# Attention with a mixture layer on one core: the written order of the first eleven stretches, replaced by another

## The chip, the core and the metric

The kernel runs on one core of a Trainium2 chip. The metric is the device time of one execution in microseconds (us); lower is better. Times of the kernel before: a median of 790.81 us over three runs (790.41 to 791.25). The engines are called by the names that the profile uses: PE (matmuls; PEld are its weight loads), DVE (vector), ACT (activation), POOL, and SP, which in this kernel only issues DMAs. ACT and POOL can issue DMAs as well.

## The reference, cut to what matters

```
xn = layernorm(A_x)                            # 2048 tokens x 640
q  = xn @ wq                                   # 32 heads of 192
k, v = the last 512 cached rows of each head   # given, not projected
p  = softmax(q @ k.T * 192**-0.5)              # per head, 2048 x 512
s  = (p @ v, heads joined) @ wo                # 2048 x 640
g  = silu(xn + the update of the two tokens with the highest xn @ w_r)   # a gated MLP on those two
out = A_x + s * g
```

Everything is bfloat16 outside the accumulators. Inputs and outputs lie in HBM.

## The kernel before, in words

**Tiles and units.** The 2048 tokens are 16 tiles of 128. Heads are taken in pairs p (two heads, 2 x 192 columns), and two pairs make a group g of four heads. A *step* i is (group, block of 512 tokens, pair): i = 0 and 1 are pairs 0 and 1 of tokens 0 to 511, i = 2 and 3 the same pairs for tokens 512 to 1023, and so on. A *unit* n is 128 tokens of a step for both heads of the pair: units 4i to 4i+3 belong to step i, 256 in all. Units are worked on in *stretches*: stretch 0 has units 0 and 1, stretch 1 units 2 and 3, and from there on each has three (stretch 2 has 4, 5, 6; stretch 10 has 28, 29, 30). There are 86.

**No scheduler.** The order on each engine is the order in which the program records its operations. Each engine runs its list strictly in that order. Semaphores let an instruction wait for data or for a buffer that another engine still holds. For stretches 11 to 84 a formula (stretch(), line 837) writes the list, the last one is the text LAST, and for the start and the stretches 0 to 10 it is written by hand as a text of tokens, FIRST (line 867). first() (line 668) turns each token into instructions. The tokens, with their lines in the profile:

- `x.t.lo.hi` loads token tiles lo to hi of block t (L101); `k`, `wq`, `v`, `wo` load keys, weights and values (L120 and L124, L112, L133, L140). A trailing `a` puts the load's issue on ACT's queue, otherwise SP issues it.
- `bn.n.h` (L172, L174 on DVE) or `as.n` (L242, L243 on ACT) take the layernorm statistics of tile n; `sq`, `rc` (L232, L235) or `pw.lo.hi` (L220 to L223 on POOL) make the reciprocal deviations; `ap.n.v` or `ap.n.g` writes the normalised tile (L260 on DVE, L258 on POOL); `sx` and `ex` load ACT's tables for square root and exponential.
- `turn.n` transposes tile n on PE (L267) and copies it out on the engine named; `kt` does so for the first keys (L282, L289; copies L283 on ACT, L290 on DVE). `xT.lo.hi` transposes normalised tiles by a DMA that SP issues (L271), and `kT.p` does it for keys (L128).
- `z.1` is a matmul on zeros that only keeps PE going at the start (L695).
- `q.i.c` is chunk c (128 columns of three) of the query projection of step i, five matmuls (L317); with lo and hi only for those tiles. A trailing `g` takes its PSUM buffer from the pool of six (p) instead of the pool of two (f). `qe` copies it out, scaled (L309 on ACT, L307 on DVE).
- `S.j` is the scores of stretch j: two matmuls of 128 rows for each unit (L331), then two of 64 rows (L338). Six p buffers are taken by three units, so S.j must wait for whatever held them last.
- `M.n.h` is the row maximum (L346, DVE), `E.n.h` the exponential with its row sum (L353, ACT), `P.n` the transpose of the exponentials by a DMA that SP issues (L358), `R.j` the reciprocals of the sums (L362).
- `O.n` is the product with the values, eight matmuls (L372), `Oe` its scaled copy (L385 on ACT, L387 on DVE), `T.j` its transpose by DMA from SP (L393).
- `W.w` is the output projection of 128 tokens for a group, twelve matmuls in two halves (L420); `We` copies it into the accumulator (L432).

**What the order has to respect.** PE, DVE, ACT, POOL and SP each have a list of their own, and a token that stands early for one engine holds up all later tokens of that engine. A DMA that SP issues waits, besides its data, for the landing of the one eight places ahead in the same list. The two f buffers are used in turn by `q`, `O` and `turn` without `g`; the next use waits for the copy-out of the last but one. Buffers of exponentials (5), their transposes (6) and attention outputs (3) are taken in turn as well.

Of the kernel before, what the change touches and what calls it, by code (L numbers as in the profile page):

```python
# [925 lines left out]
```

## Time and profile before

| | |
|---|---|
| median of the runs shown | 790.81 us (790.41 to 791.25) |
| time of the profiled execution | 789.15 us |
| its span in the profile | 787.4 us, so 1.75 us lie around it |
| mean granted PE clock | 0.999 |
| DVE busy | 621.7 us (79%) |
| ACT busy | 479.4 us (61%) |
| POOL busy | 179.5 us (23%) |
| moved by DMA | 143.80 MB, 421358 of 453133 packets under 512 B |

Busy time of PE is a union of pipelined matmuls: a matmul of 512 columns counts about 379 ns and follows the one before it after 216 ns, so a stall shorter than the rest of a matmul doesn't show as idle time. Stalls of PE are therefore read from the length of a group of equal matmuls against the same group elsewhere. A DMA's duration in the timeline is that of its issue on SP (SPq) or ACT (ACTq); the view of DMAs gives the time from issue to landing.

### The profile page before, as it was taken

How to read it: one execution, taken by the hardware profiler on the slowest of the kernel's cores; microseconds unless marked ns; L12 is line 12 of the kernel's file. 1: busy time of each engine (PE TensorE's matmuls, PEld its weight loads, DVE VectorE, ACT ScalarE, POOL GpSimd, SP SyncE). 2: the span in 40 equal slices, each digit the busy share in tenths (PEclk: the TensorE clock that was granted, in tenths of full speed). 3: DMA queues.
4: the chain of work that ended last, by engine and by line, in shares of the span. 5: the costliest groups of instructions: out<-in, count | busy, mean ns of one | idle time of the engine just before them, and what ended most of it. 6: DMA issues, size and time to landing. Idle time of an engine off the chain costs nothing.

```text
span 787.4 us, 15694 instructions
## 1 busy us (share of the span) xinstructions
PE 781.8 (99%) x5767; PEld 482.8 (61%) x5767; DVE 621.7 (79%) x1238; ACT 479.4 (61%) x1299; POOL 179.5 (23%) x198
## 2 busy tenths in 40 slices
PE   8999999999999999999999999999999999999998
PEld 4566656666666666566666655666566666556666
DVE  7976678988888777777777777777788988777786
ACT  8975766565556655565665556565667865565652
POOL 3230000000010000000000699960000000165966
PEclk9999999999999999999999999999999999999999
DMA  9999998899889999999998899779997799997996
GB/s 262 214 202 229 204 199 132 164 175 202 166 147 219 184 195 217 142 221 198 191 222 144 181 180 188 158 141 174 202 172 138 143 193 184 183 194 152 177 167 148
DMA packets 453133, 143.80 MB, mean 183 GB/s; under 512 B 421358, under 2 KB 452720, under 8 KB 453056
## 3 DMA queue, kind: packets, MB, share of 16 engines
q1 hardware_dynamic: 447696, 138.04, 94.0%
q10 hardware_dynamic: 4672, 3.08, 1.4%
q0 software_dynamic: 688, 1.68, 0.9%
q8 instruction: 45, 0.74, 0.4%
q14 instruction: 32, 0.26, 0.1%
HBM read 39.98 MB, written 2.62 MB: 54 GB/s over the span
## 4 chain that ended last, share of the span: by engine, by line
PE 95%; DMA 2%; DVE 1%; ACT 1%; issue 0%; SPq 0%; POOL 0%; DVEq 0%
PE q_ps L317 26%; PE w_ps L420 26%; PE o_ps L372 21%; PE sc L331 14%; PE sc L338 8%; DMA oT<-o_sb 1%; DMA x_in<-in_A_x_dram 1%; ACT pexp L353 1%; DVE nm L346 0%; DVE stats L172 0%; POOL fin_o L447 0%; PE gu_ps L590 0%; ACT o_sb L385 0%; PE y_ps L627 0%; DVE fin_t L445 0%
## 5 line engine op out<-in xcount | busy, mean ns | idle before, releaser
L353 ACT ACTIVATE pexp<-sc,nm 128x512 bf16<-128x512 f32 x512 | 348.5, 697 | 264.1 <-issue 231.7
L346 DVE TENSOR_REDUCE nm<-sc 128x1 f32<-128x512 f32 x512 | 314.9, 682 | 70.9 <-PE sc L338 70.7
L317 PE MATMUL q_ps<-xnT,wq_p 128*128 128x512 bf16 (+1 forms) x985 | 225.4, 374 | 0.5 <-DMA wq_p<-in_A_wq_dram 0.5
L420 PE MATMUL w_ps<-wo_g,oT 128*128 128x320 bf16 (+1 forms) x1542 | 223.0, 298 | 0.1
L420 PEld LDWEIGHTS <-oT 128*128 128x128 bf16 x1542 | 150.4, 98 | 69.5 <-DMA oT<-o_sb 0.4
L372 PE MATMUL o_ps<-v_sb,pT 128*128 128x192 bf16 x2048 | 184.8, 246 | 0.0
L372 PEld LDWEIGHTS <-pT 128*128 128x128 bf16 x2048 | 171.4, 98 | 14.0 <-issue 2.8
L317 PEld LDWEIGHTS <-wq_p 128*128 128x128 bf16 x985 | 89.7, 98 | 122.8 <-issue 33.3
L387 DVE TENSOR_TENSOR o_sb<-o_ps,lsum 128x384 bf16<-128x384 f32 x240 | 132.0, 556 | 41.3 <-PE o_ps L372 22.7
L331 PE MATMUL sc<-kT,qT 128*128 128x512 bf16 x512 | 125.5, 379 | 0.1
L434 DVE TENSOR_TENSOR s_acc<-s_acc,w_ps 128x320 f32<-128x320 f32 x192 | 92.5, 483 | 30.7 <-PE w_ps L420 30.7
L353 ACT ACTIVATION_READ_ACCUMULATOR pexp<-sc,nm 128x1 f32 x512 | 110.2, 215 | 0.0
L309 ACT ACTIVATE qT<-q_ps 128x512 bf16<-128x512 f32 (+1 forms) x180 | 98.7, 604 | 0.0
L331 PEld LDWEIGHTS <-qT 128*128 128x128 bf16 x512 | 48.5, 98 | 42.0 <-issue 1.5
L338 PE MATMUL sc<-kT,qT 64*128 64x512 bf16 x512 | 70.2, 380 | 0.0
L338 PEld LDWEIGHTS <-qT 64*128 64x128 bf16 x512 | 18.0, 94 | 46.7 <-issue 35.8
L664 POOL TENSOR_TENSOR s_acc<-s_acc,xn 128x640 f32<-128x640 f32 x16 | 22.9, 1434 | 103.0 <-DVE s_acc L434 102.9
L643 POOL TENSOR_TENSOR xn<-xn,yh 128x640 bf16<-128x640 bf16 x32 | 44.6, 1394 | 2.7
L633 POOL DMA_DIRECT2D y_d<-y_sb x4 | 2.2, 544 | 181.2 <-DVE y_sb L630 181.2
L510 POOL DMA_DIRECT2D c_d<-cand x1 | 0.7, 725 | 162.8 <-DVE cand L508 162.8
L665 POOL TENSOR_TENSOR s_acc<-s_acc,x_fin 128x640 f32<-128x640 f32 x16 | 22.4, 1400 | 61.4 <-DVE s_acc L434 54.3
L642 POOL TENSOR_SCALAR yh<-y_bc,oh 128x640 bf16<-128x640 bf16 x32 | 25.6, 800 | 5.2 <-DMA y_bc<-y_d 3.6
(110 smaller groups left out, 234.1 us busy)
## 6 DMA issues: line engine op xcount, KB each, us to landing
wo_g<-in_A_wo_dram SPq DMA_DIRECT2D x15, 480.0 KB, 4.3
wq_p<-in_A_wq_dram SPq DMA_DIRECT2D x14, 480.0 KB, 4.6
v_sb<-in_A_v_cache_dram SPq DMA_DIRECT2D x15, 384.0 KB, 4.3
k_raw<-in_A_k_cache_dram SPq DMA_DIRECT2D x28, 192.0 KB, 3.2
pT<-pexp SPq DMA_TRANSPOSE x256, 3.6
x_fin<-in_A_x_dram SPq DMA_DIRECT2D x16, 160.0 KB, 2.7
wgu<-in_B_w_gate_dram SPq DMA_DIRECT2D x15, 128.0 KB, 3.3
wgu<-in_B_w_up_dram SPq DMA_DIRECT2D x15, 128.0 KB, 3.6
```

The source lines that it names most:

```text
L309: nc.scalar.activation(out=out, in_=in_, func=ACT.Copy, scale=scale)
L317: nc.tensor.matmul(q_ps, lhsT=wq_of[g * PAIRS + pr][:, dc, c * P:(c + 1) * P], rhs=xnT[:, t5 * 4 + lo:t5 * 4 + hi, dc, :], start=(dc == 0) ...
L331: nc.tensor.matmul(sc_of[n][hh], lhsT=qT_of[i][:, 2 * hh, u * P:(u + 1) * P], rhs=kp[:, :, 2 * hh, :], start=True, stop=False)
L338: nc.tensor.matmul(sc_of[n][hh], lhsT=qT_of[i][hs, 1, u * P:(u + 1) * P], rhs=kp[hs, :, 1, :], start=False, stop=True)
L346: nc.vector.tensor_reduce(out=nm_of[j][:, c:c + 1], in_=sc_of[n][hh], axis=AX.X, op=ALU.max, negate=True)
L353: nc.scalar.activation(out=pe_of[n][:, hh, :], in_=sc_of[n][hh], func=ACT.Exp, bias=nm_of[j][:, c:c + 1], scale=1.0, accum_out=l_of[j][:, ...
L372: nc.tensor.matmul(ps[:, hh, :], lhsT=pT_of[n][:, hh, jj, :], rhs=v_sb[:, hh, jj, :], start=(jj == 0), stop=(jj == NJ - 1))
L387: nc.vector.tensor_tensor(out=osb_of[j][:, m], in0=ps, in1=l_of[j][:, 2 * m:2 * m + 2].unsqueeze(2).to_broadcast([P, 2, Dh]), op=ALU.mult)
L420: nc.tensor.matmul(w_ps, lhsT=oT_of[j][:, stretches[j].index(n), c % 3, :], rhs=wo_of[g][:, c, lo:hi], start=(c == 0), stop=(c == CPG - 1))
L434: nc.vector.tensor_tensor(out=acc, in0=acc, in1=w_ps, op=ALU.add)
L642: nc.gpsimd.tensor_scalar(out=yh, in0=M["y_bc"][:, j, :], scalar1=M["oh"][:, n, j:j + 1], scalar2=0.0, op0=ALU.mult, op1=ALU.add)
L643: nc.gpsimd.tensor_tensor(out=xn[:, n, :], in0=xn[:, n, :], in1=yh, op=ALU.add)
```

## The change

The text FIRST is replaced by another text; nothing else is. The sets of tokens agree but for details: tile 0 is turned with a p buffer and copied by ACT, tiles 2 and 3 are copied by ACT as well, and `kt.0` is copied by DVE; the load of tiles 2 and 3 is made of two loads (`x.0.2.3`, `x.0.3.4`), which stand next to each other in SP's list, so that six DMAs are issued up to `wq.0` and not five; the two loads `wo.0.0` and `wo.0.1` stand apart in the text, with no other SP token between them; loads that ACT issued (`wq.2`, `wq.3`, `v.2`, `k.3.0`, `k.3.1`, `k.2.0`, `wo.1.0`) are issued by SP; `T.9` is one DMA instead of two; tiles 12 and 15 exchange the engines of their statistics, and tiles 8, 12, 14 and 15 those that normalise them (DVE and POOL); and several copies out of PSUM change between DVE and ACT, or the buffer pool of their matmuls between f and p. Everything from stretch 11 on is recorded as before. In the diff one line is the start or a stretch:

```diff
--- before.py
+++ after.py
@@ -865,18 +865,18 @@
 
     J0 = 11
     FIRST = """
-z.1 z.1 z.1 sx z.1 z.1 x.0.0.2 x.0.2.4 as.1 k.0.1 k.0.0 bn.0.0 bn.0.1 bn.3.0 sq.0.1 sq.1.2 as.2 rc.0.1 rc.1.2 wq.0 x.1.1.2 ap.0.v ex ap.1.v bn.3.1 pw.2.4 turn.0.v turn.1.1.v kt.0.a kt.1.v q.0.0.0.2.g qe.0.0.0.2.a ap.3.g bn.5.0 x.1.0.1 x.1.3.4 x.1.2.3 q.0.1.0.2.g k.1.1 bn.5.1 qe.0.1.0.2.a q.0.2.0.2.g k.1.0 qe.0.2.0.2.a turn.3.1.a as.6 ap.2.v bn.7.0 bn.7.1 turn.2.v 
-S.0 bn.4.0 v.0 bn.4.1 wq.1 q.0.0.2.4.g qe.0.0.2.4.a x.2.0.4 kT.1 M.0.0 E.0.0 pw.4.8 q.0.2.2.4.g M.0.1 qe.0.2.2.4.v E.0.1 P.0 q.0.1.2.4 qe.0.1.2.4.a M.1.0 M.1.1 E.1.0 E.1.1 ap.4.v 
-S.1 q.1.2 ap.5.g M.2.0 ap.7.g E.2.0 M.2.1 q.1.0.2.4 ap.6.g xT.4.6 q.1.0.0.2.g bn.10.0 qe.1.2.a M.3.0 M.3.1 R.0 bn.10.1 xT.6.8 E.2.1 qe.1.0.0.2.a qe.1.0.2.4.a q.1.1 P.2 bn.11.0 O.0 bn.11.1 bn.8.0 E.3.0 E.3.1 qe.1.1.a Oe.0.v P.1 bn.8.1 
-S.2 x.3.0.4 v.1 q.2.1.0.2 as.9 M.4.0 M.4.1 q.2.0 M.6.0 E.4.0 pw.8.12 E.4.1 q.2.2.g M.5.0 qe.2.1.0.2.a E.5.0 qe.2.0.v M.6.1 ap.10.g E.6.0 ap.9.g P.3 E.6.1 M.5.1 q.3.1 qe.2.2.v ap.8.v R.1 ap.11.g O.2 qe.3.1.v Oe.2.v E.5.1 
-S.3 M.8.0 M.7.0 P.4 P.5 M.8.1 q.2.1.2.4 M.7.1 R.2 xT.8.10 M.9.0 as.13 bn.15.0 M.9.1 E.8.0 E.7.0 E.8.1 q.3.2 bn.14.0 xT.10.12 E.7.1 P.6 qe.2.1.2.4.a q.3.0.g qe.3.0.a qe.3.2.v E.9.0 E.9.1 O.1.g O.5.g O.4.g Oe.4.a Oe.1.v P.8 as.12 Oe.5.v O.3 
-S.4 P.7 bn.15.1 M.10.0 q.4.1 M.11.0 M.12.0 M.11.1 Oe.3.a q.4.0 P.9 M.10.1 qe.4.1.v E.10.0 M.12.1 E.11.0 T.0 E.11.1 q.5.0.g E.10.1 wo.0.0 wo.0.1 T.2.0.1 E.12.0 E.12.1 R.3 qe.4.0.a O.8.g O.7 P.10 Oe.7.a qe.5.0.v T.1 Oe.8.v R.4 bn.14.1 pw.12.16 
-S.5 ap.12.g O.6 M.13.0 P.11 E.13.0 M.15.1 Oe.6.a M.15.0 E.15.0 E.15.1 q.4.2 M.13.1 P.12 q.5.2.g M.14.1 M.14.0 qe.4.2.v O.9 E.13.1 Oe.9.a qe.5.2.v E.14.0 W.0 We.0.v E.14.1 
-S.6 M.17.0 P.13 M.17.1 ap.14.g M.16.1 O.10 M.18.1 Oe.10.a M.16.0 ap.13.g E.17.0 q.5.1 E.17.1 qe.5.1.v T.2.1.3 E.16.0 R.5 O.12 O.11.g Oe.11.a M.18.0 E.18.0 Oe.12.a E.16.1 W.1 O.13.g We.1.v E.18.1 ap.15.g xT.13.16 xT.12.13 W.2 We.2.v P.15 Oe.13.a 
-S.7 q.6.1 M.19.1 M.19.0 E.19.0 M.20.0 q.6.0 qe.6.0.v P.14 T.4 M.21.0 M.20.1 M.21.1 E.19.1 T.3 q.6.2.g k.2.1.a qe.6.1.a O.14 O.15.g R.6 E.20.0 q.7.1.g E.20.1 Oe.14.a P.17 qe.6.2.a E.21.0 Oe.15.v q.7.0 P.16 E.21.1 P.19 W.3 P.18 W.4 qe.7.1.v R.7 qe.7.0.v We.3.v O.19 We.4.a wq.2.a 
-S.8 wq.3.a O.16 Oe.19.v M.22.0 v.2.a M.23.1 E.22.0 Oe.16.v k.3.0.a M.23.0 P.20 E.23.0 wo.1.0.a E.23.1 k.3.1.a T.5 M.22.1 M.24.0 P.21 q.7.2 E.24.0 O.17 Oe.17.v E.22.1 P.22 k.2.0.a W.5 qe.7.2.v M.24.1 We.5.a O.20 P.23 W.6 O.21 We.6.a E.24.1 Oe.20.a Oe.21.a O.18.g Oe.18.v P.24 
-S.9 M.25.0 M.27.1 M.25.1 M.27.0 q.8.1 E.25.0 E.25.1 q.9.0 T.6 M.26.0 qe.8.1.v W.7 E.27.0 E.27.1 E.26.0 M.26.1 R.8 We.7.v P.25 qe.9.0.v E.26.1 q.8.0 T.7 
-S.10 P.27 qe.8.0.v M.28.0 E.28.0 O.22 O.23 Oe.22.a M.29.0 O.24.g P.26 q.8.2 M.28.1 M.29.1 R.9 Oe.23.v O.25 E.28.1 M.30.0 E.29.0 W.9 Oe.25.v E.30.0 E.29.1 qe.8.2.a kT.2 Oe.24.a P.28 M.30.1 kT.3 We.9.a W.8 E.30.1 We.8.v O.26.g P.29 O.27.g T.8 P.30 Oe.26.a wo.1.1 Oe.27.a v.3 T.9.2.3 T.9.0.2
+z.1 z.1 z.1 z.1 x.0.0.2 bn.0.0 x.0.2.3 sx as.1 bn.0.1 sq.0.1 sq.1.2 rc.0.1 x.0.3.4 rc.1.2 ap.0.v ap.1.v bn.3.0 k.0.0 z.1 as.2 turn.0.1.a bn.3.1 k.0.1 wq.0 turn.1.v kt.0.v kt.1.v x.1.3.4 pw.2.4 q.0.0.0.2.g ex ap.2.v q.0.1.0.2.g qe.0.0.0.2.a qe.0.1.0.2.a turn.2.a q.0.2.0.2.g ap.3.g bn.7.0 qe.0.2.0.2.a x.1.1.2 bn.7.1 turn.3.a 
+S.0 bn.5.0 bn.5.1 x.1.0.1 x.1.2.3 q.0.2.2.4.g k.1.1 as.6 bn.4.0 bn.4.1 k.1.0 M.0.0 wq.1 q.0.0.2.4.g E.0.0 v.0 M.0.1 E.0.1 qe.0.0.2.4.v qe.0.2.2.4.v x.2.0.4 q.0.1.2.4 q.1.0.0.2 qe.0.1.2.4.a qe.1.0.0.2.a pw.4.8 M.1.0 E.1.0 ap.4.v ap.5.g M.1.1 kT.1 P.0 E.1.1 
+S.1 M.2.0 q.1.2 M.3.0 bn.8.0 E.2.0 ap.7.g xT.4.6 q.1.0.2.4 q.1.1.g M.2.1 M.3.1 qe.1.0.2.4.v E.3.0 bn.8.1 bn.10.0 ap.6.g xT.6.8 qe.1.2.a E.2.1 qe.1.1.a O.0 R.0 E.3.1 bn.10.1 bn.11.0 
+S.2 bn.11.1 M.4.0 Oe.0.a q.2.1.0.2 M.5.0 qe.2.1.0.2.v q.2.0 P.2 P.1 x.3.0.4 as.9 pw.8.12 R.1 E.4.0 E.5.0 v.1 M.4.1 ap.11.g q.3.1 q.2.2.g M.5.1 ap.9.g E.4.1 M.6.1 qe.2.0.a P.3 E.5.1 M.6.0 O.2 qe.2.2.v E.6.0 ap.8.g E.6.1 P.4 Oe.2.v ap.10.g qe.3.1.v 
+S.3 M.7.0 as.15 E.7.0 q.2.1.2.4 qe.2.1.2.4.a q.3.2 M.7.1 M.9.0 M.9.1 M.8.0 O.1 E.7.1 R.2 E.9.0 qe.3.2.a bn.12.0 Oe.1.v E.9.1 M.8.1 O.3.g q.3.0.g xT.8.10 Oe.3.v xT.10.12 O.4 P.5 E.8.0 qe.3.0.v P.6 E.8.1 Oe.4.a 
+S.4 M.10.1 O.5 q.4.0 bn.14.0 as.13 Oe.5.a M.10.0 P.7 M.12.0 E.10.0 q.4.1 M.11.0 P.8 M.12.1 E.12.0 qe.4.0.v q.5.0.g M.11.1 T.0 O.7 E.10.1 qe.4.1.a E.11.0 R.3 P.9 O.8 wo.0.0 E.11.1 E.12.1 qe.5.0.v 
+S.5 Oe.7.a bn.14.1 Oe.8.v O.6 bn.12.1 wo.0.1 M.13.0 pw.12.16 M.13.1 M.15.1 R.4 T.2.0.1 P.10 M.14.0 Oe.6.v M.14.1 E.13.0 O.9 Oe.9.a E.14.0 T.1 E.13.1 ap.14.v E.14.1 q.5.2.g q.4.2 P.12 M.15.0 W.0 qe.4.2.a O.10 E.15.0 E.15.1 qe.5.2.v We.0.v ap.12.v P.11 Oe.10.v ap.15.v 
+S.6 M.16.0 M.17.0 ap.13.g M.18.1 E.16.0 q.5.1 E.17.0 T.2.1.3 O.12 M.16.1 M.17.1 E.16.1 W.2 P.13 xT.13.16 xT.12.13 M.18.0 qe.5.1.v E.17.1 We.2.v E.18.0 E.18.1 Oe.12.a W.1 O.11.g We.1.a Oe.11.v O.13 R.5 
+S.7 q.6.0 P.14 P.15 Oe.13.a q.7.0 M.19.0 E.19.0 M.19.1 E.19.1 T.3 O.15.g M.20.1 qe.6.0.a M.20.0 O.14.g q.6.1 k.2.1.a E.20.0 Oe.15.v Oe.14.a T.4 P.16 qe.7.0.a P.18 M.21.0 E.21.0 P.17 M.21.1 q.6.2.g E.20.1 P.19 W.3 qe.6.2.v qe.6.1.v R.6 E.21.1 We.3.v W.4 We.4.a 
+S.8 O.19 T.5 q.7.1 M.22.0 R.7 E.22.0 M.22.1 P.20 E.22.1 M.23.0 M.24.1 P.21 k.3.0 E.23.0 k.2.0 M.23.1 q.7.2.g O.16.g qe.7.1.a M.24.0 Oe.19.v E.24.0 k.3.1 E.23.1 Oe.16.v O.18 qe.7.2.v W.5 O.17 E.24.1 W.6 Oe.18.a We.5.a v.2 wq.3 O.21 We.6.a Oe.17.v 
+S.9 O.20 wq.2 M.25.0 R.8 M.26.0 M.25.1 Oe.21.a wo.1.0 P.22 P.23 M.26.1 E.25.0 Oe.20.v q.9.0 q.8.0.g E.26.0 P.24 E.25.1 E.26.1 qe.8.0.a M.27.0 M.27.1 W.7 We.7.v q.8.1 T.6 qe.9.0.a E.27.0 E.27.1 
+S.10 M.28.0 qe.8.1.a O.22 M.28.1 E.28.0 O.23 M.29.1 E.28.1 M.29.0 T.7 Oe.22.v q.8.2.g P.25 O.24.g M.30.0 P.26 E.29.0 P.27 M.30.1 qe.8.2.a E.29.1 E.30.0 Oe.23.v W.8 E.30.1 R.9 O.25 Oe.24.v O.26 kT.2 P.28 kT.3 P.30 T.8 W.9 We.8.a P.29 Oe.25.v Oe.26.a wo.1.1 O.27.g v.3 Oe.27.a T.9 We.9.v
     """.split()
 
     for token in FIRST:
```

## The prediction

> **What bounds the kernel now.** First the page: PE's line and the chain that ended last.
>
> ```profile
> PE 781.8 (99%) x5767; PEld 482.8 (61%) x5767; DVE 621.7 (79%) x1238; ACT 479.4 (61%) x1299; POOL 179.5 (23%) x198
> ...
> PE 95%; DMA 2%; DVE 1%; ACT 1%; issue 0%; SPq 0%; POOL 0%; DVEq 0%
> ```
>
> PE is the bound, and the change gives it the same matmuls. So only PE's waits up to stretch 11 can be won or lost. The view of busy time by windows shows how little room that is.
>
> ```profile
> core 0: us, PE busy (x) PEld busy (x) DVE busy (x) ACT busy (x) POOL busy (x), PEclk, DMA share, GB/s
> 0.00:10.88 10.88, 8.97 (x67) 5.04 (x67) 6.76 (x23) 8.46 (x19) 3.11 (x13) 1.00 0.86 261
> 10.88:20.11 9.23, 9.14 (x63) 4.88 (x61) 9.13 (x23) 8.85 (x26) 4.46 (x8) 1.00 1.15 261
> 20.11:34.26 14.15, 14.15 (x101) 8.11 (x100) 14.08 (x30) 13.28 (x37) 4.59 (x9) 1.00 1.12 226
> ...
> 98.45:787.40 688.95, 685.48 (x5086) 425.71 (x5083) 546.67 (x1080) 403.15 (x1091) 160.81 (x150) 1.00 0.95 177
> ```
>
> S.0 starts at 10.88 and S.11 at 98.45. From 10.88 to 34.26 PE, DVE (23.21 of 23.38 us) and ACT (22.13) are all full, and the DMA share is over 1: any of them can stop PE there. The granted clock is full throughout.
>
> PE's waits come from its timeline, by comparing equal groups.
>
> ```profile
> 8.61 1.81 PE L317 MATMUL q_ps<-xnT,wq_p 128*128 128x256 bf16 x15 [0.45 <-DMA wq_p<-in_A_wq_dram]
> ...
> 10.88 1.03 PE L331 MATMUL sc<-kT,qT 128*128 128x512 bf16 x4
> ...
> 12.38 1.81 PE L317 MATMUL q_ps<-xnT,wq_p 128*128 128x256 bf16 x15
> 14.02 1.36 PE L331 MATMUL sc<-kT,qT 128*128 128x512 bf16 x4
> ...
> 15.85 3.62 PE L317 MATMUL q_ps<-xnT,wq_p 128*128 128x512 bf16 x20
> 19.45 0.82 PE L372 MATMUL o_ps<-v_sb,pT 128*128 128x192 bf16 x8
> ...
> 26.70 1.46 PE L331 MATMUL sc<-kT,qT 128*128 128x512 bf16 x6
> ...
> 34.26 1.80 PE L331 MATMUL sc<-kT,qT 128*128 128x512 bf16 x6
> ...
> 41.38 1.68 PE L331 MATMUL sc<-kT,qT 128*128 128x512 bf16 x6
> ...
> 47.24 1.79 PE L420 MATMUL w_ps<-wo_g,oT 128*128 128x320 bf16 x12
> ...
> 51.69 1.24 PE L317 MATMUL q_ps<-xnT,wq_p 128*128 128x512 bf16 x5
> 52.76 1.48 PE L372 MATMUL o_ps<-v_sb,pT 128*128 128x192 bf16 x16
> 54.08 2.02 PE L420 MATMUL w_ps<-wo_g,oT 128*128 128x320 bf16 x12
> ...
> 80.82 1.62 PE L331 MATMUL sc<-kT,qT 128*128 128x512 bf16 x6
> ```
>
> S.1 takes 1.36 where S.0 took 1.03: 0.33 lost. The four projections from 15.85 to 19.45 take 3.60; two of 1.07 (51.69 to 52.76) and two of 0.55 (three from 12.38 to 14.02) make 3.24: 0.36 lost. Six score matmuls take 1.46 undisturbed, so S.4 loses 0.34, S.5 0.22 and S.9 0.16. W.1 loses 0.23 against W.0. That is 1.64 us in all, 0.21% of 789.15; and about 0.2% (1.6 us) is what a measurement of this kernel can tell from no change. The whole prize of these stretches is one such step, while a loss has no ceiling.
>
> **The change part by part.** The prices, from the timelines of DVE, ACT and POOL:
>
> ```profile
> 8.20 0.42 DVE L290 COPY kT<-tp_k 128x512 bf16<-128x512 bf16 x1
> 9.05 1.00 ACT L283 COPY kT<-tp_k 128x1024 bf16<-128x1024 bf16 x1
> 9.38 0.87 POOL L258 TENSOR_SCALAR xn<-x_in,rstd,nmr 128x640 bf16<-128x640 bf16 x1
> 10.10 0.39 DVE L260 TENSOR_SCALAR xn<-x_in,mv,rstd 128x640 bf16<-128x640 bf16 x1
> 10.80 0.69 ACT L268 COPY xnT<-tp 128x640 bf16<-128x640 bf16 x1
> 11.80 0.88 DVE L172 BATCH_NORM_STATS2 stats<-x_in 128x6 f32<-128x320 bf16 x2
> 13.98 0.41 DVE L307 TENSOR_SCALAR qT<-q_ps 128x256 bf16<-128x256 f32 x1
> 14.18 0.68 ACT L353 ACTIVATE pexp<-sc,nm 128x512 bf16<-128x512 f32 x1
> 15.51 0.77 DVE L260 TENSOR_SCALAR xn<-x_in,mv,rstd 128x640 bf16<-128x640 bf16 x1
> 22.14 2.43 DVE L346 TENSOR_REDUCE nm<-sc 128x1 f32<-128x512 f32 x4
> ```
>
> *Start to S.0: +0.1.* Before, q.0.0 starts at 8.61, when wq.0 lands. wq.0 is now the sixth issue, some 0.5 us later, but behind the same bytes; I keep 8.6. The price of kt.0 on DVE is not in the trace, which has it on ACT alone (1.00); DVE's row for half the size (0.42) bounds it from below. I take 0.7, since that row is nearest in kind. Then kt.1 is out at 9.2 and ap.2 at 9.6. bn.3 now stands behind ap.0 and ap.1, so POOL's ap.3, which began at 9.38, ends at 10.5. ACT's list runs qe.0.0, qe.0.1 (10.2), the copy of tile 2 (0.69), qe.0.2, the copy of tile 3. S.0's second matmul needs qe.0.2, ready near 11.2, and S.0 ends at 12.5 where it ended at 12.38. With the two ends for kt.0 this term lies between -0.2 and +0.4.
>
> *S.1: -0.33.* q.1.0.0.2 now stands ahead of S.1, and its 0.55 us of PE's work cover the copies for which S.1 waited. Its weights, wq.1, are now issued ahead of v.0 and land earlier than before.
>
> *q.1.2 to O.0: -0.36, and +0.23 back.* Other f and p buffers remove the old waits. But on DVE ap.4 (0.77 beside POOL) now stands ahead of M.1.1, so that E.1.1 starts only at 16.55. ACT takes E.1.1, E.2.0 and E.3.0 (spaced by 0.66) and then qe.1.2 (0.6): 19.13. O.0 needs that f buffer; PE would be there at 18.90.
>
> *q.3.1: +0.43.* A new wait. q.3.1 reuses the f buffer of q.2.1.0.2, whose copy stands on DVE behind bn.11.1, M.4.0 and M.5.0. DVE's list from M.0.0 (12.7) through that copy is ten maxima (0.60 each by the four in 2.43), three pairs of statistics with their aggregates (1.04), four half copies (0.33 by spacing), ap.4 (0.7) and R.0 (0.1): 11.2 us, so 23.9, with the buffer free at 24.0. PE arrives at 23.57. Behind q.3.1 wait q.2.2 and O.2, and so S.3. With a start 0.3 earlier or later this wait is 0.1 or 0.75.
>
> *S.4, S.5, S.9: -0.34, -0.22, -0.16.* S.4's buffers now come from E.8, E.9, Oe.3 and qe.3.0; the last is due at 34.55 for a matmul at 34.56, and as.13 stands behind all of ACT's. S.5 no longer needs Oe.8, and T.0, for which Oe.8 had to wait, is issued one transpose earlier. S.9's last buffers come from We.6, and the whole of O.21 lies between.
>
> *W.1: -0.23.* T.2.1.3, the transpose that it waited for, is issued ahead of P.13, one place earlier.
>
> *Single copies that change engines, T.9 as one DMA, the two wo.0 loads:* nothing. Behind 41 us DVE and ACT have idle time that takes them; T.9 is not read before stretch 12; the wo.0 loads stay neighbours in SP's list. If that cover is gone, one copy costs about 0.4.
>
> Sum: 0.1 - 0.33 - 0.36 + 0.23 + 0.43 - 0.34 - 0.22 - 0.16 - 0.23 = **-0.88 us**; with the ends of the two uncertain terms -1.5 to -0.3. Against the profiled 789.15 that is 788.27. The median of the runs shown is 1.66 above the profiled execution, and I carry that difference over: 790.81 - 0.88, about **789.9** (own range 789.3 to 790.5).
>
> **Transposes by DMA** decide the next case. First SP's timeline, then the view of DMAs for three windows (28.4 to 28.6, 31.4 to 31.6, and 34.70 to 35.95, whose GB/s stand in 40 slices).
>
> ```profile
> 29.98 2.97 SPq L271 DMA_TRANSPOSE xnT<-xn  x2
> ```
>
> ```profile
> pT<-pexp SPq DMA_TRANSPOSE x1, 3.8
> ...
> xnT<-xn SPq DMA_TRANSPOSE x1, 5.3
> ...
> GB/s 238 295 762 205 172 156 221 205 180 123 41 66 106 33 8 8 16 8 0 0 0 0 0 0 0 0 0 0 0 0 0 0 8 8 8 8 8 8 8 8
> ...
> q8 instruction: 1, 0.02, 4.7%
> ```
>
> P.5, issued in the first window, lands 3.8 us later. The second xT, issued in the next one, needs 5.3 and lands near 36.8. The third shows why: an instruction load passes on q8, and nothing moves for most of a microsecond. [...]
>
> **The rivals.**
>
> *P.5 is caught: +1.0.* P.5 now takes the place of the second xT, issued near 31.6 and due near 35.4. O.5 needs it directly after S.4, at 35.85. If the instruction load comes before P.5 has landed, P.5 lands near 36.85, PE loses 1.0 and the total is +0.1, **790.9**. For it: the same place in SP's list was hit. Against it: the load came while PE was at the third matmul of S.4; by the count of matmuls that is now the last but one of S.4, near 35.5.
>
> *Slower: the seven loads in SP's list.* Timelines of SP, ACT's issues and PE:
>
> ```profile
> 70.26 2.12 SPq L358 DMA_TRANSPOSE pT<-pexp  x1
> ...
> 70.57 1.13 ACTq L112 DMA_DIRECT2D wq_p<-in_A_wq_dram  x2
> ...
> 78.20 5.22 SPq L358 DMA_TRANSPOSE pT<-pexp  x3
> ...
> 83.12 2.33 PE L317 MATMUL q_ps<-xnT,wq_p 128*128 128x512 bf16 x10
> ```
>
> ACT issued these loads, wq first, from 70.57 on, while SP went from P.21 (70.26 to 72.38) to P.22 (78.20). Now SP issues all seven between the two, wq.3 and wq.2 fifth and sixth. Their 2.39 MB at the 261 GB/s of the first window take 9.2 us, from 73 to 82.2; wo.1.0 is the last 1.8, so wq.2 lands by 80.4 and P.22 by 84. q.9.0 takes the place in time of 83.12, less 0.88: 82.2; q.8.0 needs wq.2 at 83.3. S.10 needs the buffer of E.27.0, and that needs P.22, by 87. The mechanism decides from about 2.9 us more delay on. The most I grant is the gap in SP's list, 72.38 to 78.20, 5.8 us; less 2.9 it costs 2.9, and with -0.88 that is +2.0, **792.8**. [...] No run so far shows these loads in SP's list.
>
> *More is gained than the profiled run shows.* If the 1.66 us between profiled and timed runs are waits in these stretches and the new order removes most of them, -0.88 becomes -2.3, **788.5**. Nothing in the trace shows such waits.
>
> **How the numbers follow.** Forecast 0.46, P.5 caught 0.20, slower by SP's list 0.24, more gained 0.10. Faster by over 0.2%: the last case and 0.04 of the forecast, in which the two added waits don't come, 0.14. Slower: 0.24, and 0.02 of P.5's case: 0.26. Within: 0.60. The range goes from 788.9, between the fourth case and the forecast (0.06 below), to 793.1, the third case with a start that is 0.3 late (0.12 above).
>
> **What would show it.** In the changed profile: the projection behind S.0 at 12.5; S.1's four matmuls in 1.03; q.3.1 late, at 24.0; S.4 in 1.46, and a gap ahead of O.5 or none; T.2.1.3 landed before W.2 needs it; S.11 at 97.6, and from there 688.95 us as before. The forecast is wrong if S.11 starts after 98.5, or if PE waits at q.9.0, q.8.0 or in S.10.

## The result, and the profile after

The changed kernel takes 792.16 us (median of 16 runs, 790.57 to 793.59) against 790.25 of the kernel before (16 runs, 789.21 to 791.47): a ratio of 1.0023, 95% interval 1.0016 to 1.003. That is 1.9 us slower, where 0.9 less was forecast. Timed anew (after_again) it gave 1.0022 (1.0013 to 1.0031). The profiled execution has a span of 789.3 us, 1.9 above that of before.

First the page of the changed kernel: PE's line, the chain that ended last, and the two groups of matmuls that now wait.

```profile
PE 781.5 (99%) x5767; PEld 482.7 (61%) x5767; DVE 620.2 (79%) x1238; ACT 479.8 (61%) x1297; POOL 177.8 (23%) x196
...
PE 93%; DMA 3%; ACT 1%; issue 1%; DVE 1%; SPq 0%; POOL 0%; DVEq 0%; ACTq 0%
...
L420 PE MATMUL w_ps<-wo_g,oT 128*128 128x320 bf16 (+1 forms) x1542 | 223.0, 298 | 0.6 <-DMA oT<-o_sb 0.6
...
L372 PE MATMUL o_ps<-v_sb,pT 128*128 128x192 bf16 x2048 | 185.4, 246 | 1.0 <-DMA pT<-pexp 1.0
```

The same two groups on the page of before:

```profile
L420 PE MATMUL w_ps<-wo_g,oT 128*128 128x320 bf16 (+1 forms) x1542 | 223.0, 298 | 0.1
...
L372 PE MATMUL o_ps<-v_sb,pT 128*128 128x192 bf16 x2048 | 184.8, 246 | 0.0
```

PE has the same work; 2% of the chain went from PE to DMAs and to "issue". What the matmuls wait for now are transposes by DMA. To see where, cut both spans at S.0, S.11 and S.13 (view of busy time by windows; columns as in the prediction). Before, behind the first window, which the prediction shows:

```profile
10.88:98.45 87.57, 87.33 (x621) 52.00 (x619) 68.22 (x137) 67.83 (x193) 15.54 (x35) 1.00 1.13 217
98.45:114.30 15.85, 15.85 (x120) 9.71 (x117) 12.02 (x23) 11.15 (x32) 0.00 (x0) 1.00 1.16 202
114.30:787.30 673.00, 669.62 (x4969) 416.00 (x4967) 534.65 (x1058) 392.00 (x1059) 160.81 (x150) 1.00 0.94 176
```

After:

```profile
0.00:11.16 11.16, 9.20 (x67) 5.15 (x67) 6.88 (x23) 8.49 (x19) 3.12 (x13) 1.00 0.84 248
11.16:98.80 87.64, 86.25 (x622) 52.07 (x620) 66.44 (x136) 68.91 (x191) 13.98 (x33) 1.00 1.11 213
98.80:116.25 17.45, 16.40 (x118) 9.43 (x117) 12.24 (x24) 10.92 (x30) 0.00 (x0) 1.00 1.11 200
116.25:789.25 673.00, 669.62 (x4969) 416.07 (x4967) 534.59 (x1057) 391.47 (x1059) 160.72 (x150) 1.00 0.95 177
```

S.0 is 0.28 later, S.0 to S.11 takes 0.07 more, S.11 to S.13 takes 1.60 more, and behind S.13 nothing differs. So most of the loss lies in stretches 11 and 12, **whose recorded order the change doesn't touch**. PE's timeline shows each wait in brackets:

```profile
8.95 1.27 PE L317 MATMUL q_ps<-xnT,wq_p 128*128 128x256 bf16 x10 [0.68 <-DMA wq_p<-in_A_wq_dram]
...
15.05 1.03 PE L331 MATMUL sc<-kT,qT 128*128 128x512 bf16 x4
...
23.59 3.41 PE L317 MATMUL q_ps<-xnT,wq_p 128*128 128x512 bf16 x15 [0.80 <-DMA xnT<-xn]
...
34.34 1.46 PE L331 MATMUL sc<-kT,qT 128*128 128x512 bf16 x6
...
37.11 0.83 PE L372 MATMUL o_ps<-v_sb,pT 128*128 128x192 bf16 x8 [0.56 <-DMA pT<-pexp]
...
42.34 1.46 PE L331 MATMUL sc<-kT,qT 128*128 128x512 bf16 x6
...
54.16 3.02 PE L420 MATMUL w_ps<-wo_g,oT 128*128 128x320 bf16 x21
...
104.31 1.40 PE L420 MATMUL w_ps<-wo_g,oT 128*128 128x320 bf16 x9 [0.63 <-DMA oT<-o_sb]
...
115.58 0.83 PE L372 MATMUL o_ps<-v_sb,pT 128*128 128x192 bf16 x8 [0.42 <-DMA pT<-pexp]
```

S.1's four matmuls take 1.03, S.4's and S.5's six take 1.46: the old waits are gone. The brackets count idle time only; counted from matmul start to matmul start the new waits are 0.97 at 23.59 (q.2.0), 0.72 at 37.11 (O.5), 0.80 at 104.31 (a W, for T.8) and 0.73 in stretch 12, for the transposes of stretch 11's exponentials (0.15 at 114.33 and 0.58 at 115.58). The chain of waits from 96 to 118 us names the two late ones:

```profile
100.84 3.43 DMA oT<-o_sb
...
104.31 0.78 PE w_ps L420 x5
...
112.19 3.35 DMA pT<-pexp
...
115.58 0.83 PE o_ps L372 x8
```

T.8 was issued at 100.84 and landed at 104.27. Why so late? SP's timeline after:

```profile
73.91 1.99 SPq L124 DMA_DIRECT2D k_raw<-in_A_k_cache_dram  x3
...
78.32 8.03 SPq L358 DMA_TRANSPOSE pT<-pexp  x3
86.45 3.60 SPq L393 DMA_TRANSPOSE oT<-o_sb  x2
90.15 4.04 SPq L358 DMA_TRANSPOSE pT<-pexp  x3
94.25 1.54 SPq L128 DMA_TRANSPOSE kT<-k_raw  x1
...
100.84 1.35 SPq L393 DMA_TRANSPOSE oT<-o_sb  x1
...
106.20 7.29 SPq L358 DMA_TRANSPOSE pT<-pexp  x3
```

and before:

```profile
83.51 1.31 SPq L393 DMA_TRANSPOSE oT<-o_sb  x1
...
98.39 1.34 SPq L393 DMA_TRANSPOSE oT<-o_sb  x1
...
105.00 5.83 SPq L358 DMA_TRANSPOSE pT<-pexp  x3
```

P.22 to P.24, behind the seven loads, take 8.03 us to issue (P.22 alone 4.09), and T.6 is issued at 86.45 instead of 83.51: 2.94 late. From 78.32 on each row begins within 0.1 of the end of the one before it. **The list has no pause in which to catch up**, so at T.8 it is still 2.45 late (100.84 instead of 98.39). Before, T.8 landed at 101.82, 1.34 ahead of the place where PE needs it (4.71 behind S.11); after, it lands 0.76 behind that place. The second wait is for P.33, the last transpose of stretch 11. P.31 to P.33 are issued from 106.20 instead of 105.00 and take 7.29 us instead of 5.83, so that P.33 lands at 115.53 (112.98 before), for a matmul at 115.58.

### The profile page after: what moved, and what is told of

The parts are those of the page before. It is cut to its first block, busy times and chain, and to the rows that moved or that the text cites. A ratio compares the mean times of both kernels' runs of the same rounds, so it can differ in the third digit from the quotient of the medians.

```text
span 789.3 us, 15694 instructions
## 1 busy us (share of the span) xinstructions
PE 781.5 (99%) x5767; PEld 482.7 (61%) x5767; DVE 620.2 (79%) x1238; ACT 479.8 (61%) x1297; POOL 177.8 (23%) x196
## 4 chain that ended last, share of the span: by engine, by line
PE 93%; DMA 3%; ACT 1%; issue 1%; DVE 1%; SPq 0%; POOL 0%; DVEq 0%; ACTq 0%
PE w_ps L420 26%; PE q_ps L317 25%; PE o_ps L372 21%; PE sc L331 13%; PE sc L338 8%; DMA pT<-pexp 1%; ACT pexp L353 1%; DMA wq_p<-in_A_wq_dram 1%; DMA x_in<-in_A_x_dram 1%; DMA oT<-o_sb 0%; POOL fin_o L447 0%; PE gu_ps L590 0%; SPq L358 0%; DVE nm L346 0%; ACT qT L309 0%
## 5 line engine op out<-in xcount | busy, mean ns | idle before, releaser
L387 DVE TENSOR_TENSOR o_sb<-o_ps,lsum 128x384 bf16<-128x384 f32 x244 | 134.4, 557 | 40.7 <-PE o_ps L372 22.7
L309 ACT ACTIVATE qT<-q_ps 128x512 bf16<-128x512 f32 (+1 forms) x183 | 101.1, 606 | 0.4 <-PE q_ps L317 0.2
```

What stands on the lines that cost most here:

```text
L309: nc.scalar.activation(out=out, in_=in_, func=ACT.Copy, scale=scale)
L387: nc.vector.tensor_tensor(out=osb_of[j][:, m], in0=ps, in1=l_of[j][:, 2 * m:2 * m + 2].unsqueeze(2).to_broadcast([P, 2, Dh]), op=ALU.mult)
```

## The experiments

Theory Q: the seven loads in SP's list make all later transposes late, and PE pays in stretches 11 and 12. Rivals: an instruction load makes the waits (F, I), the order of stretch 10 does (O), the early waits do (E, G), or loads in flight stop transposes whatever their queue (C). The expectation of after_again tells theory V and rival L. All edits are to the text FIRST; SP's order is the order of its tokens. The table has the times and, from the one profiled execution of each, the three parts that can differ (S.13 to the end is the same but for 0.4). Each ratio is to runs of the kernel before that were timed beside it, whose medians go from 789.81 to 790.50; the medians of two rows are therefore compared by their ratios. "+need" has SP's last list by need, "+P.5" P.5 early, "+x" one load for x.0's tiles 2 and 3.

| kernel | median us | ratio to before, interval | S.0 | S.0 to S.11 | S.11 to S.13 |
|---|---|---|---|---|---|
| before | 790.25 | | 10.88 | 87.57 | 15.85 |
| before_again | 790.35 | 1.0007 (0.9998 to 1.0016) | 11.17 | 88.30 | 15.84 |
| changed | 792.16 | 1.0023 (1.0016 to 1.003) | 11.16 | 87.64 | 17.45 |
| after_again | 792.30 | 1.0022 (1.0013 to 1.0031) | 11.57 | 88.78 | 18.42 |
| loads_on_act | 796.61 | 1.008 (1.0067 to 1.0093) | 11.11 | 93.37 | 15.85 |
| loads_on_pool | 800.40 | 1.0133 (1.0119 to 1.0148) | 11.59 | 99.54 | 15.84 |
| before_loads_on_sp | 791.02 | 1.0009 (1.0 to 1.0018) | 11.00 | 88.11 | 17.11 |
| early_half | 794.45 | 1.0061 (1.0048 to 1.0074) | 12.09 | 94.21 | 15.84 |
| late_half | 790.32 | 1.0008 (0.9999 to 1.0016) | 10.98 | 87.86 | 16.57 |
| p5_first | 791.66 | 1.0019 (1.001 to 1.0027) | 11.25 | 87.36 | 17.64 |
| old_start | 792.19 | 1.0021 (1.001 to 1.0031) | 11.54 | 87.67 | 17.71 |
| t8_early | 792.86 | 1.0036 (1.0024 to 1.0049) | 11.79 | 87.76 | 17.97 |
| sp_by_need: +need | 791.61 | 1.0015 (1.0006 to 1.0024) | 11.35 | 88.32 | 15.93 |
| sp_by_need_p5: +need +P.5 | 791.36 | 1.0016 (1.0006 to 1.0025) | 11.37 | 87.22 | 16.07 |
| need_p5_again: the same | 791.11 | 1.001 (1.0001 to 1.0019) | 11.26 | 88.03 | 16.51 |
| old_start_need_p5 | 790.95 | 1.0007 (0.9998 to 1.0016) | 11.27 | 87.68 | 16.74 |
| need_p5_x: +need +P.5 +x | 790.71 | 0.9998 (0.9989 to 1.0007) | 11.49 | 87.58 | 16.69 |
| need_p5_x_again: the same | 790.57 | 1.0003 (0.9994 to 1.0012) | 11.02 | 88.38 | 17.16 |
| need_p5_x_wo | 791.24 | 1.0011 (1.0002 to 1.002) | 11.14 | 88.43 | 16.22 |
| late_by_need | 790.40 | 1.0005 (0.9996 to 1.0014) | 11.01 | 87.98 | 16.26 |

### How far one execution can be trusted

No edit: the kernel before and the changed kernel once more.

> The kernel before, unchanged, timed against itself: how far two sets of runs of one kernel lie apart, and a second profile of it. Ratio 1.000 within 0.001. If the profile shown (787.4) was a lucky execution, the second has S.11 at 99.0 to 99.5 rather than 98.45, or a wait of PE in stretch 12, and a span of 788 to 789; if not, it has S.11 at 98.3 to 98.6 and 787.4.

> The changed kernel, unchanged, timed anew, with a second profile. Ratio 1.002 to 1.003. Theory V (the loss has an early part that differs between executions: the start, q.2.0's and O.5's transposes caught by instruction loads, about even with the 1.64 won, and a late part that is steady, 1.5 in stretches 11 and 12): S.0 at 11.1 to 12.1, waits of 0.4 to 1.0 ahead of q.2.0 and 0.7 to 1.2 ahead of O.5, S.11 at 98.6 to 99.7, and again 17.4 to 17.6 from S.11 to S.13. Rival L (the late waits are no steady part): S.11 to S.13 in 15.9 to 16.6.

The kernel before against itself gives 1.0007, within its interval of 1, and a span of 788.4 instead of 787.4: S.11 at 99.47, nothing late behind it. So the profile that the prediction was made from was an execution 1 us quicker than the typical one, all of it ahead of S.11. The changed kernel's second profile by windows:

```profile
11.57:100.35 88.78, 86.79 (x621) 51.85 (x619) 66.30 (x136) 68.96 (x191) 14.21 (x33) 1.00 1.09 209
100.35:118.77 18.42, 16.53 (x119) 9.43 (x118) 12.24 (x24) 11.04 (x30) 0.00 (x0) 1.00 1.14 196
```

against the second one of before:

```profile
99.47:115.31 15.84, 15.84 (x118) 9.69 (x117) 12.02 (x23) 11.13 (x32) 0.00 (x0) 1.00 1.13 207
```

S.11 to S.13 is 15.84 or 15.85 before and 17.45 or more in all four profiles that keep the changed order from stretch 8 on behind the changed stretches 3 to 7 (changed, after_again, p5_first, old_start). In after_again the early waits came as theory V has them (0.68 ahead of q.2.0, 1.09 ahead of O.5), but S.11 at 100.35 was later than 99.7, and the late part of 18.42 was 0.8 above the 17.4 to 17.6 expected. So the late part is no steady 1.5; rival L, by which it could fall to 16.6, is further off.

### Where the loads are issued

loads_on_act puts the seven loads back into ACT's list, loads_on_pool into POOL's, before_loads_on_sp moves them into SP's in the kernel before. A "ring" in the expectations is a queue of the views of DMAs: q1 holds what SP issues, q10 what ACT issues.

```diff
-S.8 ... P.21 k.3.0 E.23.0 k.2.0 ... k.3.1 E.23.1 ... v.2 wq.3 ...
-S.9 O.20 wq.2 ... wo.1.0 P.22 ...
+S.7 ... wq.2.a
+S.8 O.19 wq.3.a ... v.2.a E.22.0 ... k.3.0.a E.23.0 ... k.3.1.a wo.1.0.a E.23.1 ... k.2.0.a E.24.1 ...
```

> The changed kernel with the seven loads (wq.2, wq.3, v.2, k.3.0, wo.1.0, k.3.1, k.2.0) back in ACT's list at the places that they had before; all else as changed. Theory Q (these loads in SP's list make every later transpose some 2.5 us late, and PE pays for it in stretches 11 and 12): P.22's issue, which took 4.09 us, takes under 2; T.8, landed at 104.27, lands by 102; the waits of PE at 104.31 (0.80) and at 113.5 to 115.6 (0.77) go; S.11 stays near 98.8; the time is the changed one less 1.6, 790.6. Rival F (the second wait comes from the instruction load at 107.81 and from T.9 being one transpose, not from the loads): only the first wait goes, 791.4. Rival O (the order of the transposes in stretch 10): both stay, 792.2.

> The changed kernel with the seven loads issued by POOL, which has no other work from 50 to 115, at the same places of the order; SP has only transposes there and no engine that computes stands behind a load's wait. Theory Q (the SP list and its ring are what is late): P.22 follows P.21 within 2 us, T.8 lands by 102, no wait in stretches 11 and 12; 790.6. Rival C (loads from any queue stop the transposes that are on their way, as they did from ACT's, where P.20 took 7.5 us to land and P.21 8.8): P.21 and P.22 land 6 us or more after their issue, PE waits for them in stretches 8 and 9, 793 or more.

> The kernel before with the same seven loads moved from ACT's list into SP's, between P.21 and P.22, in the order that the changed kernel has; all else as before. Theory Q: P.22 and all transposes behind it are 2 to 3 us late, T.8 lands near 104 where it landed at 101.82, PE waits in stretches 11 and 12 although their code and all of the order are as before; S.11 at 98.45 to 98.6, and the time is 1.2 to 1.9 above the kernel before, near 791.8. Rivals F and O: no change, 790.2.

With ACT the late waits do go (15.85), but S.0 to S.11 takes 5.7 us more than in the changed kernel. A PE that comes to S.11 so late would give even a late list time to land, so neither this 15.85 nor the 15.84 of loads_on_pool is a test of theory Q. ACT's timeline of loads_on_act:

```profile
79.63 0.69 ACT L353 ACTIVATE pexp<-sc,nm 128x512 bf16<-128x512 f32 x1 [3.13 <-DMA pT<-pexp]
...
84.23 0.69 ACT L353 ACTIVATE pexp<-sc,nm 128x512 bf16<-128x512 f32 x1 [3.82 <-DMA pT<-pexp]
```

PE's timeline of the same kernel:

```profile
83.65 0.98 PE L372 MATMUL o_ps<-v_sb,pT 128*128 128x192 bf16 x8 [2.77 <-DMA pT<-pexp]
```

P.20 and P.21, issued 0.1 and 1.6 us behind the first of ACT's loads, took 8.8 and 11.8 us from issue to landing. Two of the loads stood in ACT's list waiting for them, with exponentials queued behind, and PE waited 2.9 us. From POOL it is worse. PE's timeline in loads_on_pool:

```profile
65.23 4.68 PE L420 MATMUL w_ps<-wo_g,oT 128*128 128x320 bf16 x21 [9.62 <-DMA oT<-o_sb]
```

and SP's:

```profile
53.41 6.43 SPq L358 DMA_TRANSPOSE pT<-pexp  x1
59.94 7.08 SPq L271 DMA_TRANSPOSE xnT<-xn  x2
```

POOL, which has nothing to wait for, issued five of the loads between 47.56 and 51.7, and transposes that SP issued behind them landed late: PE's matmul at 65.23 waits for T.2.1.3, issued 14 us earlier at 51.15, the issue of P.13 alone takes 6.43 and its landing 12.6, and PE waits 9.6 us, in stretch 6 and not in 8 and 9 as expected. Rival C is right here: behind loads from another queue the transposes came too late for PE. So the old place of the loads can't simply be restored in the new order. In the kernel before, ACT's loads met P.20, T.5 and P.21 as well, but all three had been issued ahead of them; the slowest, P.21, took 7.0 us and still had 2.3 to spare (landed at 77.23 for O.21 at 79.50).

before_loads_on_sp is the clean test of Q, as nothing else moves. S.11 to S.13 takes 17.11, 1.27 more, all of it waits in stretch 12 (0.38, 0.21 and, for P.33 at 115.55, 0.62); T.8 landed at 103.78, just in time. The time is 0.6 above before (0 to 1.4), under the 1.2 to 1.9 expected. Q has the right place and sign; its size in time is smaller than in the profile, and the interval reaches down to no change.

### Halves of the change

early_half has the changed order to the end of stretch 7 and the old one behind it; late_half the reverse.

```diff
-S.7 ... W.4 We.4.a
+S.7 ... W.4 We.4.a q.7.1.g qe.7.1.v R.7 O.19 wq.2.a
```

> The changed order up to the end of stretch 7, then the order before for stretches 8 to 10 (loads in ACT's list again, the two halves of T.9 again). Theory Q (the loss is made by SP's list from stretch 8 on): no wait of PE in stretches 11 and 12 (S.11 to S.12 and S.12 to S.13 are 7.93 and 7.92), and the time is that of the kernel before plus what the first stretches give, between -0.3 and +0.4: 790.1 to 790.8. Rival E (the early waits ahead of q.2.0 and O.5 are the loss): as slow as the changed kernel, 791.8 or more. A danger to both is that ACT's loads meet transposes that are now issued at another moment, as when they alone were put back (796.6).

> The order before up to the end of stretch 7, then the changed order for stretches 8 to 10. Theory Q: PE waits in stretch 11 for T.8 and in stretch 12 for a pT, 0.7 to 1.6 in all, with S.11 near 98.5 to 99; the time is 0.8 to 1.6 above the kernel before, 791.2 to 792.0. Rival E: 790.4.

early_half met the danger that its expectation named: T.5 and P.21, issued 0.5 and 2.2 us behind the first of ACT's loads, took 9.3 and 11.4 us to land.

```profile
80.96 2.58 PE L420 MATMUL w_ps<-wo_g,oT 128*128 128x320 bf16 x9 [3.04 <-DMA oT<-o_sb]
```

Its S.11 to S.13 is 15.84, but S.0 to S.11 takes 6.6 us more than in the changed kernel, which could have covered a late list as in loads_on_act; so it tells little. late_half has T.8's wait (0.71) and no second one, and comes out 0.5 us above before, less than expected and hardly measurable. Behind the old start the changed stretches 8 to 10 cost about that; behind the changed one, 1.6 and more.

### The early waits, and T.8 alone

```diff
-S.3 ... xT.8.10 Oe.3.v xT.10.12 O.4 P.5 E.8.0 ...
+S.3 ... P.5 xT.8.10 Oe.3.v xT.10.12 O.4 E.8.0 ...
```

old_start takes the first four lines of the text from before, with P.4 at their end; t8_early has `T.8` ahead of `kT.3`.

> The changed kernel with P.5 issued ahead of xT.8.10 and xT.10.12, where it stood before. The wait of PE ahead of O.5 (0.72 at 37.11) goes, and S.5 starts near 41.6 instead of 42.34. Theory Q: S.11 comes up to 0.7 earlier, but PE then waits so much longer for T.8, since SP's list behind the seven loads is what is late; the time stays within 0.2 of the changed kernel, 792.0. Rival G (each wait of PE adds up, wherever it is): 0.7 less, 791.4.

> The changed kernel with the first four lines of the order (up to the end of stretch 2) as they were before, and P.4 at their end. S.0 is at 10.88 again, xT.6.8 lands near 21.9 so that q.2.0 doesn't wait (0.97), but S.1 and the projections ahead of O.0 wait again (0.33 and 0.36); S.3 starts near 26.7 instead of 27.50. Theory Q: what is won is waited for again at T.8, the time stays within 0.2 of the changed kernel, 792.0. Rival G: the 0.6 to 0.8 carries to the end, 791.4.

> The changed kernel with T.8 issued one place earlier, ahead of kT.3, whose scores come only in stretch 12. T.8 lands near 102.7 instead of 104.27: the wait of PE at 104.31 (0.80) falls to 0.1 or less. Theory Q: the wait for a pT in stretch 12 (0.73) stays or takes a part of what is won, since v.3 and T.9 are as late as before; 791.4 to 792.0. Rival G (each wait counts by itself): 0.8 less, 791.4.

p5_first removes O.5's wait, but the xT behind P.5 is now late (0.46 ahead of q.4), so that S.5 starts at 41.95 and not at 41.6; S.11 comes 0.19 earlier and the late part takes 0.19 more. The ratio fell by 0.0004 (0.3 us), which lies between Q and G and within the noise. old_start has no wait at q.2.0, but O.5's grew to 1.17 and the time stayed. So p5_first's profile fits Q, its time tells neither from G, and old_start, whose early waits didn't shrink as meant, tests neither. t8_early removed T.8's wait and made a longer one, 2.1 us, for P.29:

```profile
108.26 1.49 PE L372 MATMUL o_ps<-v_sb,pT 128*128 128x192 bf16 x16 [1.94 <-DMA pT<-pexp]
```

P.29, still the last of these transposes, was in flight when an instruction load passed on q8 at 105.8; from 106.3 to 107.5 all queues together moved 8 to 64 GB/s, and PE went on at 108.26. The expected 791.4 to 792.0 missed that.

### SP's last list in the order of need

```diff
-S.10 ... kT.2 P.28 kT.3 P.30 T.8 W.9 ... P.29 ... wo.1.1 O.27.g v.3 Oe.27.a T.9 We.9.v
+S.10 ... kT.2 P.28 T.8 P.30 P.29 kT.3 W.9 ... O.27.g Oe.27.a We.9.v T.9 wo.1.1 v.3
```

> The changed kernel with SP's last list in the order in which PE needs it: kT.2, P.28, T.8, P.30, P.29, kT.3, T.9, wo.1.1, v.3 (it was kT.2, P.28, kT.3, P.30, T.8, P.29, wo.1.1, v.3, T.9). The loads of stretch 8 stay where the change has them. Theory Q: T.8 and P.29 land by 103 and 104, T.9 by 109, ahead of their use, so PE's waits of 0.80 and 0.73 go and S.13 starts 17.3 after S.11 minus 1.5, that is 15.85 after it: 790.6. Rival I (an instruction load then stops other transposes of the same list, as it did with P.29 when only T.8 was moved): one wait of 1 to 2 us appears in stretch 11 or 12 and the time stays at 791.5 to 792.5.

> The same with P.5 ahead of the two xT of stretch 3 as well. Theory Q: now that nothing waits for SP behind stretch 10, the 0.2 to 0.4 that P.5 brings by S.9 carries to the end: 790.3. Rival I: as for the kernel without it, 791.5 or more.

> The changed kernel with P.5 early and SP's last list by need, once more: its profiled execution (787.7) was far below its median. Theory V: the late part stays without a wait above 0.3 (S.11 to S.13 15.9 to 16.3), and the difference comes early: S.11 at 99.0 to 100.0 where it was at 98.59, from the start and from q.2.0; median 791.0 to 791.6. Rival L: a wait of 1 or more in stretch 11 or 12, S.11 at 98.6.

> The same with x.0 loaded by one issue for its tiles 2 and 3 (x.0.2.4, as before) instead of two, so that wq.0 and all loads behind it are issued 0.5 us earlier. Theory V: q.0.0 starts 0.3 earlier and S.0 with it, near 11.0; 0.3 less than without it, 790.9. If the start is covered by something else (the second tile's statistics, which then wait for a longer load): S.0 stays at 11.3 or later, 791.2 or more.

> The best version so far once more: whether it is level with the kernel before (0.9998, 0.9989 to 1.0007). Theory V: ratio 0.999 to 1.001, S.3 starts 15.5 to 15.9 after S.0 since q.2.0 doesn't wait, one wait of 0.5 to 0.9 for a pT in stretch 12.

> The changed kernel with SP's last list by need, P.5 early, x.0's tiles 2 and 3 by one issue, and wo.1.1 issued behind T.7 instead of behind T.9, so that only v.3 stands ahead of P.31. If the load ahead of P.31 makes the last wait (0.78 in stretch 12), it falls by 0.3 to 0.6 and S.13 starts 16.1 to 16.4 after S.11; T.8, 0.6 us later, is still ahead of its use; 790.3, level with the kernel before or 0.3 under it. If the instruction load alone makes it, it stays at 0.7 and the time at 790.7.

> The first four lines of the order (to the end of stretch 2) as before, the changed order behind them, P.5 early, SP's last list by need. Theory V: S.0 at 10.9 to 11.2, no wait at q.2.0, but the waits in S.1 and ahead of O.0 (0.33, 0.36) again; the gains behind S.3 (S.4, S.5, W.1, S.9: 0.95) remain, no late wait: 790.0 to 790.5, the kernel before or up to 0.3 under it. Rival L: 791 or more.

> The order before up to the end of stretch 7, the changed order for stretches 8 to 10, and SP's last list by need as above. Theory Q: the wait of 0.71 that the changed stretches 8 to 10 had behind this start goes, and the time is 789.6 to 790.0, equal to the kernel before or up to 0.4 faster. Rival I: 790.5 or more.

The seven loads stay where the change has them; only what SP does behind P.28 is turned round. The late part of sp_by_need by windows:

```profile
99.67:115.60 15.93, 15.93 (x118) 9.64 (x117) 12.14 (x24) 10.92 (x30) 0.00 (x0) 1.00 1.09 208
```

PE is busy throughout, as before the change. That shows the place: T.8 and P.33, late in SP's list, made PE wait in stretches 11 and 12. Over the five profiles with the list by need and no other change behind stretch 2 but P.5 (sp_by_need to need_p5_x_again, without old_start) S.11 to S.13 takes 15.93 to 17.16; what remains is a wait for a pT behind v.3 (0.1 to 0.8), and once one for kT.3 (0.47). In time the list alone gives 0.0008 of the ratio back, which the intervals don't separate from nothing: 791.61 us is far from the 790.6 of theory Q and within rival I's range, though its profile has no late wait. sp_by_need_p5 (790.3 expected, 791.36 measured), old_start_need_p5 (790.0 to 790.5, 790.95) and late_by_need (789.6 to 790.0, 790.40) came out slower than expected too. With P.5 and one load for x.0 as well, the kernel is level with the one before (0.9998 and 1.0003): all of the loss is gone, 0.0022 of the ratio, and nothing is won. Which of the three edits gave how much isn't shown: the two profiles of this kernel still have 0.8 and 1.3 us of the late loss. need_p5_x_wo, with wo.1.1 away from P.31, has no wait for a pT in stretch 12, as its first theory expected, but an O waits for its pT in stretch 10 instead (0.56 at 95.71), and the time is no better (790.3 expected). No version beats the kernel before.

need_p5_x meant to make S.0 earlier. The three profiles with the changed start and one load have 11.49, 11.02 and 11.14, those with two loads 11.11 to 12.09, so a gain is likely but not shown. The one load took away q.2.0's wait in all three; in need_p5_x:

```profile
22.57 3.96 PE L317 MATMUL q_ps<-xnT,wq_p 128*128 128x256 bf16 x20
```

In the changed kernel an instruction load on q14 passes at 22.1, ahead of q.2.0's wait. Whether the one load of x.0 moves it was not shown.

## Why the prediction was wrong, step by step

- **What bounds: right.** PE's waits were all there was to win. The sum of 1.64 was taken from one execution; before_again has other sizes (S.5 0.72 instead of 0.22), so each term was known only to some tenths.
- **Start, +0.1: mis-sized.** It is +0.28 at the start of S.0 and +0.48 at its end (the next projection at 12.86 instead of 12.38), since S.0 itself waits 0.19 for qe.0.2; the upper end was 0.4. I kept wq.0's landing at 8.6 "behind the same bytes"; q.0.0 started at 8.95. Over ten profiles with the changed start S.0 lies at 11.11 to 12.09, mean 11.45, over seven with the old one at 10.88 to 11.54, mean 11.12: +0.33, less than either spread.
- **S.1 -0.33, S.4 -0.34, S.5 -0.22, S.9 -0.16, W.1 -0.23: right.** S.1 takes 1.03, S.4, S.5 and S.9 1.46; W.2 and W.1 run 21 matmuls without a gap at 54.16.
- **Projections ahead of O.0, -0.36 and +0.23:** the old waits went. The wait of O.0 did not come in the first profile. It came with 0.50 in after_again and 0.56 in need_p5_again, but not as worked out: the profile puts it down to an exponential, yet P.0 landed at 20.13 and 19.71, each 0.05 ahead of O.0, while qe.1.2, on which the term rests, had ended 0.66 and 0.72 ahead of it.
- **q.3.1, +0.43: the wrong wait.** PE stopped earlier, at q.2.0, for an xT (0.97). I had looked at instruction loads near 35 us only. The view of DMAs from 21.5 to 23.6 (40 slices of 52 ns) has one on q14:

```profile
GB/s 162 117 74 78 181 185 185 107 88 102 210 293 395 244 258 215 44 59 68 20 5 10 5 10 5 10 5 10 10 5 10 5 10 15 185 288 297 283 297 288
...
q14 instruction: 1, 0.01, 0.9%
```

  From 22.5 to 23.2 almost nothing moves (5 to 20 GB/s).
- **Rival "P.5 is caught", +1.0: it happened,** with 0.72 here (the load passed on q8 at 34.6, and from 35.2 to 36.4 at most 20 GB/s moved) and 0.74 to 1.17 in the other profiles with P.5 late. It deserved more than its chance of 0.20: no profile with the changed place of P.5 is without it. These two steps explain S.0 to S.11: -0.98 forecast, +0.54 at q.2.0, +0.72 at O.5, -0.23 for O.0's wait that didn't come, makes +0.05; measured +0.07. Two small stalls of like size are left out of this sum, the 0.19 inside S.0 and, before, 0.17 at 36.82.
- **The step that failed: "from S.11 688.95 us as before".** It is 690.50. "T.9 is not read before stretch 12" was true and no reason: what matters is when T.8 and the transposes behind T.9 are issued. The term that I put at nothing is 1.55: 0.80 for T.8 and 0.73 in stretch 12, for P.33 above all.
- **Rival "seven loads in SP's list": the right mechanism at the wrong place.** P.22 by 84 was 86.05, 0.9 behind the last of the loads that stand ahead of it (wo.1.0, issued at 77.69, 7.5 us to landing); wq.2 by 80.4 was 83.81. I let the delay decide at S.10, "from about 2.9 us more delay on"; P.22 landed 2.05 behind my 84 and before the 87 of need, so PE didn't wait in S.10. For wq.2 it waited in some profiles (0.21 in after_again, 0.37 in t8_early), not in this one. I didn't follow it further down the list, where T.8 had only 1.34 to spare. Its price of 2.9 came to 1.6 (1.8 and 1.9 in p5_first and old_start, 2.6 in after_again). That its net of +2.0 is near the measured 1.9 is chance: it is the sum of a smaller late loss and of an early gain that didn't come.

**Left open.** Why wq.0 lands later in the changed start: taking the extra issue away gave S.0 at 11.02 to 11.49, and the old start itself spreads over 10.88 to 11.54. And why before_loads_on_sp loses 1.27 in its profiled execution between S.11 and S.13 but only 0.6 (0 to 1.4) in time; the timed executions have no trace here that could tell.

## What to carry to other kernels

When DMAs are moved into another queue, follow the delay down that queue until its first pause, not to the first reader that might miss it; a queue without pauses hands the delay on, and the reader with the least to spare pays, here 26 us later in code that was not changed. Compare the landing of each transfer with the moment of its use, and write such a queue in the order of need. Where the stakes are tenths of a microsecond, take two profiles of the same kernel before pricing a wait: here they differed by 1 us.
